# Reordering the first head pair's units, another split of a division, two copies on ScalarE and larger adds on GpSimd in an attention and gate kernel

## Chip, cores and metric

One core of a Trainium2 chip. The metric is device microseconds of one execution, read as the median of several. Profiles give spans from the first to the last recorded instruction, which are about 2 us shorter than the time.

## The reference

```python
xn = layernorm(x)                                # x: 2048 x 640, bf16
q  = (xn @ wq)                                   # 32 heads of 192
s  = softmax(q @ k[-512:].T * 192**-0.5) @ v[-512:]   # per head, the last 512 cached positions
s  = s.reshape(2048, 32*192) @ wo
g  = silu((silu(xn @ w_gate) * (xn @ w_up)) @ w_down)
return x + s * g
```

## The kernel before

The gate `g` is computed first. Then the 32 heads go in 16 pairs. For each pair there is a phase of queries and scores, and after it a "stretch" of context and output units. The 2,048 rows are four blocks (0 to 3), each with two halves of context, `a` and `b`. The names in the order below are: `2a0` is the first half-unit of block 2's context half `a`; `2w`, `2x` and `2y` are output projections done in block 2's place, of the block two places earlier: first two row tiles, last two row tiles, and the rest columns of all four. `0e` is one query unit. Below, `w` and `x` units are called row units and `y` units rest units. Accumulators (`mm` and `sc` in the timelines) are the PSUM buffers that a unit's matmuls write and VectorE or ScalarE empties.

```python
def pv(i, q2):                     # context of block i, half q2
    ...
            st["acc"] = sc_tile() if i < 2 and q2 else mm_tile()   # two buffers each
    ...
            if p == 3:
                divide(i, q2, acc, (0, 1) if i < 2 and q2 else ())  # by VectorE, else ScalarE

def divide(i, q2, acc, by_dve):
    nc.vector.reciprocal(r[:], ...)
    ...                             # O_b = acc * r, on VectorE or ScalarE
    nc.sync.dma_start_transpose(out=OT_b[:, 6*q2 : 6*q2+6, :], in_=O_b[:, 2*q2 : 2*q2+2, :, :])

def sum_rows(i, qts, sc):          # end of a row unit
    ...
    add_sum(pr, to, sc)            # first pair: copy out of PSUM on VectorE; later: add

FIRST = """0a0 0b0 0a1 0b1 0e0 1b0 1a0 1b1 2b0 1a1 2b1 2w0 2x0 2w1 2a0 2x1 2a1 2y0 3a0 3y0 3a1 3x0
    3b0 3x1 3w0 3b1 3w1"""
...                                 # before the last pair's end: x onto the sums, on GpSimd
for qt in range(4):
    add_x(n, slice(qt, qt + 1))
add_x(n)
```

A projection needs the transposed context `OT_b` of the block that it projects: `2w` needs what half `a` of block 0 gave, `2x` what half `b` gave, `2y` both.

The softmax here doesn't subtract the row's maximum and nothing guards it: scores larger than these inputs give would overflow.

## Time and profile before

| | before |
|---|---|
| time, first three runs | 922.93 us (922.89 to 923.27) |
| span of the profiled execution | 921.8 us |
| TensorE busy | 914.7 us, 99% |
| VectorE, ScalarE, GpSimd busy | 65%, 51%, 10% |
| first pair's stretch (first context half-unit to the next query unit) | 190.74 to 210.40: 19.66 us |

A timeline row has the start, the length, the engine, the source line, the operation, output and input, how many instructions it merges, and in brackets how long the engine sat idle before it and what ended that. Matmul rows overlap, since their ends are modelled. So work is sized from start to start. Idle time of an engine other than TensorE costs nothing by itself. The rows of before stand in the prediction.

### The profile page before, as it was taken

How to read it: one execution, taken by the hardware profiler on the slowest of the kernel's cores; microseconds unless marked ns; L12 is line 12 of the kernel's file. 1: busy time of each engine (PE TensorE's matmuls, PEld its weight loads, DVE VectorE, ACT ScalarE, POOL GpSimd, SP SyncE). 2: the span in 40 equal slices, each digit the busy share in tenths (PEclk: the TensorE clock that was granted, in tenths of full speed). 3: DMA queues.
4: the chain of work that ended last, by engine and by line, in shares of the span. 5: the costliest groups of instructions: out<-in, count | busy, mean ns of one | idle time of the engine just before them, and what ended most of it. 6: DMA issues, size and time to landing. Idle time of an engine off the chain costs nothing.

```text
span 921.8 us, 23762 instructions
## 1 busy us (share of the span) xinstructions
PE 914.7 (99%) x10193; PEld 527.3 (57%) x10193; DVE 594.6 (65%) x844; ACT 473.7 (51%) x841; POOL 91.0 (10%) x302
## 2 busy tenths in 40 slices
PE   9999999999999999999999999999999999999998
PEld 5444445564747464656565656565656565555664
DVE  6443321467676777777777767676767676767656
ACT  4222222546464656565655565655556565556561
POOL 0000000000000000000000000000000000002977
PEclk9999999999999999999999999999999999999999
DMA  9312430045443425343534453435353434333535
GB/s 310 68 34 65 90 78 1 1 67 121 51 112 47 111 56 104 58 103 58 108 58 108 57 109 57 97 58 97 69 95 65 92 75 76 89 70 108 127 48 163
DMA packets 246969, 77.45 MB, mean 84 GB/s; under 512 B 227792, under 2 KB 246864, under 8 KB 246864
## 3 DMA queue, kind: packets, MB, share of 16 engines
q1 hardware_dynamic: 245376, 74.23, 39.3%
q8 instruction: 80, 1.31, 0.6%
q10 hardware_dynamic: 1488, 1.70, 0.6%
q14 instruction: 25, 0.20, 0.1%
HBM read 39.06 MB, written 2.62 MB: 45 GB/s over the span
## 4 chain that ended last, share of the span: by engine, by line
PE 98%; DMA 1%; DVE 0%; SPq 0%; POOLq 0%; POOL 0%; issue 0%; DVEq 0%
PE mm L460 22%; PE sc L474 18%; PE sc L619 16%; PE mm L499 16%; PE sc L282 11%; PE mm L321 6%; PE sc L587 3%; PE sc L579 2%; PE mm L551 2%; PE mm L579 1%; DMA x_t<-in_A_x_dram 1%; DMA OT_b<-O_b 1%; PE gu L282 0%; PE mm L330 0%; PE sc L551 0%; PE sc L499 0%
## 5 line engine op out<-in xcount | busy, mean ns | idle before, releaser
L478 ACT ACTIVATE p_t<-sc 128x1024 bf16<-128x1024 f32 x254 | 253.3, 1024 | 120.2 <-PE sc L474 120.2
L465 DVE TENSOR_REDUCE qT<-mm 128x512 bf16<-128x1024 f32 x189 | 231.2, 1223 | 98.9 <-PE mm L460 96.4
L529 ACT ACTIVATE O_b<-mm,r 128x192 bf16<-128x192 f32 x490 | 166.5, 423 | 190.4 <-issue 138.9
L460 PE MATMUL mm<-xnT,wq_p 64*128 64x512 bf16 x1890 | 234.9, 376 | 0.0
L474 PE MATMUL sc<-qT,khat 64*128 64x512 bf16 x1524 | 195.4, 376 | 0.0
L619 PE MATMUL sc<-wo_p,OT_b 64*128 64x512 bf16 (+1 forms) x1608 | 179.2, 345 | 1.2 <-DMA OT_b<-O_b 1.2
L499 PE MATMUL mm<-V_p,p_t 64*128 64x193 bf16 x3520 | 178.3, 242 | 0.0
L499 PEld LDWEIGHTS <-p_t 64*128 64x128 bf16 x3584 | 155.0, 93 | 34.6
L460 PEld LDWEIGHTS <-wq_p 64*128 64x128 bf16 x1890 | 91.8, 94 | 112.0 <-issue 0.7
L632 DVE TENSOR_TENSOR s_m<-s_m,sc 128x1024 f32<-128x1024 f32 x82 | 100.2, 1222 | 49.3 <-PE sc L619 43.0
L474 PEld LDWEIGHTS <-khat 64*128 64x128 bf16 x1536 | 74.8, 94 | 91.0
L619 PEld LDWEIGHTS <-OT_b 64*128 64x128 bf16 x1608 | 75.6, 94 | 46.2 <-DMA OT_b<-O_b 1.7
L605 POOL MEMSET turn_t<- 128x1 f32 x246 | 24.4, 99 | 699.1 <-PE mm L499 494.2
L290 DVE TENSOR_TENSOR hT<-sc,sg 128x512 bf16<-128x512 f32 x46 | 31.7, 692 | 81.6 <-ACT sg L289 81.6
L632 DVE TENSOR_TENSOR s_t<-s_t,sc 128x512 f32<-128x512 f32 x82 | 56.2, 686 | 18.3 <-PE sc L587 16.8
L289 ACT ACTIVATE sg<-sc 128x512 bf16<-128x512 f32 x46 | 27.4, 597 | 69.7 <-PE sc L282 68.2
L282 PE MATMUL sc<-xnT,wg_sb 128*128 128x512 bf16 (+1 forms) x260 | 60.2, 354 | 0.1
L282 PE MATMUL sc<-xnT,wu_sb 128*128 128x512 bf16 (+1 forms) x260 | 60.2, 354 | 0.0
L632 DVE TENSOR_TENSOR s_o<-s_o,sc 128x640 f32<-128x640 f32 x52 | 42.7, 821 | 15.9 <-PE sc L619 14.8
L321 PE MATMUL mm<-wd_sb,hT 128*128 128x512 bf16 (+1 forms) x240 | 46.7, 347 | 0.0
L518 DVE RECIPROCAL r<-mm 128x4 f32<-128x4 f32 x124 | 22.6, 182 | 33.1 <-PE mm L499 24.7
L282 PEld LDWEIGHTS <-wu_sb 128*128 128x128 bf16 x285 | 27.0, 98 | 27.1 <-issue 0.3
(94 smaller groups left out, 458.9 us busy)
## 6 DMA issues: line engine op xcount, KB each, us to landing
wo_p<-in_A_wo_dram SPq DMA_DIRECT2D x16, 480.0 KB, 4.9
K_p<-in_A_k_cache_dram SPq DMA_DIRECT2D x32, 192.0 KB, 4.6
V_p<-in_A_v_cache_dram SPq DMA_DIRECT2D x32, 192.0 KB, 3.1
wq_p<-in_A_wq_dram SPq DMA_DIRECT2D x64, 80.0 KB, 2.9
wq_p<-in_A_wq_dram SPq DMA_DIRECT2D x16, 160.0 KB, 3.2
x_t<-in_A_x_dram SPq DMA_DIRECT2D x14, 160.0 KB, 3.1
OT_b<-O_b SPq DMA_TRANSPOSE x124, 2.7
wd_sb<-in_B_w_down_dram SPq DMA_DIRECT2D x1, 1920.0 KB, 11.8
```

The lines of the kernel that those rows point to most:

```text
L282: nc.tensor.matmul(out, w_sb[:, c, f * P : (f + 1) * P], xnT[:, c, qc], start=(c == 0), stop=(c == NC - 1),)
L290: nc.vector.tensor_tensor(hTs[b][:, f, :], u, sg[:], ALU.mult)
L321: nc.tensor.matmul(dn, at, by, start=(f == 0), stop=(f == NF - 1))
L460: nc.tensor.matmul(q_ps[:, h, :], pairs[pr]["wq"][r, c, j * P : (j + 1) * P], xnT[r, c, b * 512 : (b + 1) * 512], start=(c == 0), stop=(c ...
L465: nc.vector.reduce_sum(qTs[i][:, j, :], q_ps[:, :, :].rearrange("p h n -> p n h"), axis=AX.X)
L474: nc.tensor.matmul(sc[:, h, :], khat[r, j, ks], qT[r, j, :], start=(j == 0), stop=(j == 2))
L478: nc.scalar.activation(p_t[:, :, :], sc[:, :, :], ACT.Exp, scale=scale)
L499: m = nc.tensor.matmul(acc[:, k, h * 256 : h * 256 + Dh + 1], Ps[i][kc][r, h, qt * P : (qt + 1) * P], V_p[r, kc, h, 0 : Dh + 1], start=(p ...
L529: nc.scalar.activation(O_b[:, qt, h, :], a_k[:, h, 0:Dh], ACT.Copy, scale=r[:, k, h, :])
L579: nc.tensor.matmul(ps, OTs[i][:, 3 * qt + j, :], pairs[i // NB]["wo"][:, j, cols], start=(first and j == 0), stop=(end and j == 2),)
L619: m = nc.tensor.matmul(ps[:, k, 0 : cols.stop - cols.start], OTs[i][r, 3 * qt + j, :], pairs[i // NB]["wo"][r, j, cols], start=(turn == 0 ...
L632: nc.vector.tensor_tensor(to, to, ps, ALU.add)
```

## The change

The intent is to have more work between a context half and the projection that needs its transpose, and to spread what empties the accumulators over VectorE and ScalarE. The matmuls stay the same, 10,193.

```diff
-                divide(i, q2, acc, (0, 1) if i < 2 and q2 else ())
+                divide(i, q2, acc, (0, 1) if q2 == i else ())
...
-        add_sum(pr, to, sc)
+        if i < 2 and qts.start:
+            nc.scalar.copy(to, sc)
+        else:
+            add_sum(pr, to, sc)
...
-    FIRST = """0a0 0b0 0a1 0b1 0e0 1b0 1a0 1b1 2b0 1a1 2b1 2w0 2x0 2w1 2a0 2x1 2a1 2y0 3a0 3y0 3a1 3x0
-        3b0 3x1 3w0 3b1 3w1"""
+    FIRST = """0a0 0b0 0a1 0b1 0e0 1a0 1b0 1a1 2a0 1b1 2a1 2w0 2b0 2w1 2b1 2y0 2x0 3a0 2x1 3w0 3a1 3w1
+        3x0 3b0 3x1 3b1 3y0"""
...
-                            for qt in range(4):
-                                add_x(n, slice(qt, qt + 1))
+                            for qt in (0, 2):
+                                add_x(n, slice(qt, qt + 2))
```

## The prediction

> **What bounds the kernel now.** I read the page's first part, then TensorE's waits, the chain that ended last and the timeline, and only then the other engines around the gap that these showed. The page's busy line, then all of TensorE's matmul waits:
>
> ```profile
> PE 914.7 (99%) x10193; PEld 527.3 (57%) x10193; DVE 594.6 (65%) x844; ACT 473.7 (51%) x841; POOL 91.0 (10%) x302
> ```
>
> ```profile
> PE sc L619 <- DMA OT_b<-O_b: 1.2, 1, 1.2
> PE gu L230 <- DVE zero_t L179: 1.2, 1, 1.2
> PE tp L344 <- DVE xn L267: 0.2, 1, 0.2
> ```
>
> TensorE is busy for 914.7 of 921.8 us, and the mean granted clock is 1.000. Only one wait lies in the middle: an output projection waited for a transposed context tile, once. The other two belong to the start. So this change can win about that wait and no more. The chain there (start, length, what):
>
> ```profile
> 195.32 0.57 PE mm L499 x13
> 195.89 4.62 DMA OT_b<-O_b
> 200.51 0.05 issue
> 200.55 1.47 PE sc L619 x12
> ```
>
> and TensorE's timeline over the same microseconds:
>
> ```profile
> 195.82 0.83 PE L499 MATMUL sc<-V_p,p_t 64*128 64x193 bf16 x16
> 196.49 2.17 PE L499 MATMUL mm<-V_p,p_t 64*128 64x193 bf16 x48
> 198.49 0.81 PE L619 MATMUL sc<-wo_p,OT_b 64*128 64x512 bf16 x6
> 200.55 1.47 PE L619 MATMUL sc<-wo_p,OT_b 64*128 64x512 bf16 x12 [1.25 <-DMA OT_b<-O_b]
> 201.86 0.83 PE L499 MATMUL mm<-V_p,p_t 64*128 64x193 bf16 x16
> ```
>
> Rows overlap by the modelled ends, so I size units by start to start: 16 context matmuls 0.67 us, 6 projection matmuls 0.65 us, and 10 query matmuls 1.08 us (the chain's lengths). The unit that began at 198.49 should have been followed at 199.14; the next began at 200.55. Loss 1.41 us. Check by the whole stretch of the first pair, from 190.74 to 210.40: 19.66 us for 16 context half-units (10.67), 10 projection half-units (6.47) and one query unit (1.08), together 18.22. The difference is 1.44 us, so this is the only gap in the stretch. The later pairs repeat every 46.96 us in the chain (232.79, 279.75, 326.71 ...), with no wait listed.
>
> Why was the transpose late? The transposes took this long to land, and the second, issued at 195.89, is the 4.6:
>
> ```profile
> DMA to landing us min/median/max: 2.7/2.8/4.6
> ```
>
> The transfer rate from 198.5 to 200.0 in 40 slices (busy tenths of the 16 engines, GB/s):
>
> ```profile
> DMA  0000000000000101001010010010049999999999
> GB/s 0 0 0 0 0 0 0 7 7 7 7 7 7 14 7 14 7 7 14 7 14 7 7 14 7 7 14 7 14 102 273 259 287 280 294 214 267 300 287 287
> ```
>
> A trickle of about 7 GB/s until 199.6: nearly all of the tile had moved before 198, and one straggler finished late. The one instruction packet of these microseconds (queue q8, 0.02 MB) moves just before 198.
>
> **What the Trainium skill says.** "Runtime: NRT & Kernel Launch", Instruction fetch mechanics, says that instructions are streamed by DMA in 16 KiB blocks while the engine runs; the page's 80 instruction packets with 1.31 MB agree in size (16 KB each). "DMA: Bandwidth & Descriptors", Queues, rings and completion order, says that each DMA engine alternates between its queues packet by packet: a 16 KB packet ahead of small transpose packets on one engine would make this tail. The trace fits, but does not prove it. "VectorE: DVE Perf Modes", The TRN2 errata, gives ScalarE 172 cycles plus one per element from PSUM at 1.2 GHz; for 1,024 columns that is an estimate of 1.00 us. The exponentials of that shape in this trace take 1.024 us, so I use 1.02 for the moved copies; VectorE's take 1.22. "GPSIMD Engine Reference", section 3.1, charges a GpSimd instruction a dispatch beside its per-element cost, so fewer, larger adds are cheaper. The trace agrees: 1.11 us start to start for 512 columns, 2.1 for 1,024.
>
> **The change, part by part.** No matmul is added or removed (the instruction lists have the same length). Four things move.
>
> (1) Order. Before, the second half of block 0's context was needed at 199.14, two projection half-units of 0.65 us before the next block's. Now the rest unit, which needs it first, stands after two more half-units of context and one more of projection. Laying the new list from 190.74 with the sizes above: 1a at 194.49, 1b 195.16, 2a1 ends 198.49, first projection (needs the first half) 198.49, 2b0 199.14, 2w1 199.81, 2b1 200.46, rest unit 201.12, second row unit 201.77, stretch over at 208.97. The second half is divided by ScalarE: VectorE first does the first half (reciprocal 192.95, two products to 194.18), so the second's reciprocal ends at 194.39, ScalarE needs 1.36, and the transpose is issued at about 195.8, as before. Landed after 2.8 us: 198.6; after 4.6 again: 200.4. Wanted at 201.12. The gap of 1.41 goes even if the straggler stays.
>
> (2) VectorE divides the first half of block 0 instead of the second. The next user of that accumulator starts at 194.49; VectorE is done at 194.18, ScalarE would be at 194.52. Cost 0, margin 0.3.
>
> (3) Two of the four row copies (1.22 us on VectorE) go to ScalarE (1.02 us each). ScalarE is idle there; VectorE loses 2.44 us of work. Nothing on the path, but buffers matter. The second row unit reuses the bank pair of the first; VectorE's copy of the first starts 0.20 us after its slot ends (before: slot end 201.86, copy 202.06), so 200.66 to 201.88, plus 0.05 to release TensorE. Wanted at 201.77. New wait: 0.16 us. After that shift the next reuse (rest unit's copy and add on VectorE, to about 203.5) is wanted at 203.89, fine. The last one (second rest unit: copy and add 209.33 to 210.75) is wanted by the second scores of the next pair at 210.86: margin 0.06 us after the release, so 0 to 0.1 us.
>
> (4) GpSimd adds x in four instructions of 1,024 columns instead of eight of 512:
>
> ```profile
> 880.30 4.50 POOL L657 TENSOR_TENSOR s_m<-s_m,x_b 128x512 f32<-128x512 f32 x4
> 885.86 4.50 POOL L657 TENSOR_TENSOR s_m<-s_m,x_b 128x512 f32<-128x512 f32 x4
> 890.31 1.16 POOL L657 TENSOR_TENSOR s_t<-s_t,xT 128x512 f32<-128x512 f32 x1
> 896.74 2.35 POOL L719 TENSOR_TENSOR x_b<-s_f,s_m 128x1024 bf16<-128x1024 f32 x1 [5.26 <-DVE s_f L718]
> ```
>
> Two large ones took 4.21 us for the same shape of multiply, so 0.29 is saved twice, 0.6 us. But GpSimd then idles 5.26 us for VectorE: worth 0.
>
> Sum: 1.41 - 0.16 - 0.05 = 1.2 us saved; 922.93 - 1.2 = 921.7.
>
> **Rivals.** *The gap belongs to the profiled run only.* The profiled execution took 923.57, the timed ones 922.93. With the usual 2.8 us the old transpose would land at 198.7, before 199.14, and there would be nothing to win: the change would leave 923.0 or 923.1. For it: a straggler is chance. Against: instruction packets come at fixed places of the program. I give it one in five. *A new wait takes the old one's place.* The bank reuse at 201.77 or the accumulator at 194.49 could cost more than I reckon, if VectorE runs late: each slip of VectorE's queue by 0.3 us costs at most that. It would make 922.0 to 922.5. The straggler could also hit another transpose, but every other one has over 0.6 us of slack. *The GpSimd adds were in the end's chain.* Its last step is a GpSimd add, but the 5.26 us of idle time before say no. If the idle reading were wrong, 0.6 us more would go: 921.1. *A bound of another kind* (a 2% change is 18 us) would need a stage that today has no wait at all to stall repeatedly; the later pairs are untouched.
>
> **Range and chances.** Weighing 921.7 against the one in five for 923.0, I predict 921.8. The range 921.0 to 922.9 holds no change at its top and the gap plus half the GpSimd time at its bottom. All of it is within 2%: chances 0.005 faster, 0.99 same, 0.005 slower.
>
> **What would show it.** Right: TensorE's waits lose the wait on the context transpose; the first pair's stretch is 18.3 to 18.5 us instead of 19.66; a short wait of 0.1 to 0.2 us on VectorE's copy stands before the second row unit; ScalarE's two copies show about 1.02 us; GpSimd's adds are done earlier and its idle time before the final adds grows by that. Wrong: the transpose wait stays or another of its size appears there; the stretch is short but the time isn't (then the gap never was in the timed runs); or the last chain after TensorE's end changes length.

## The result, and the profile after

The changed kernel took 921.67 us (median of six runs, 921.56 to 922.19), the kernel before 922.98 us in the same rounds (922.75 to 923.27). The ratio is 0.9986, with a 95% interval of 0.9973 to 0.9999: "same" at the threshold of 2%. A ratio here is the mean time of one kernel's fast runs over that of the other's of the same rounds, so it is not quite the ratio of the medians.

TensorE's waits in the changed kernel, all of them (waiting, releaser, total us, times, longest):

```profile
PE gu L230 <- DVE zero_t L179: 1.2, 1, 1.2
PE sc L282 <- ACT xnT L350: 0.3, 1, 0.3
```

The wait on the transpose is gone. Both lines that are left lie in the first microseconds. TensorE's timeline of the changed kernel from the first projection on, whose counterpart are the rows from 198.49 in the prediction:

```profile
197.88 0.81 PE L619 MATMUL sc<-wo_p,OT_b 64*128 64x512 bf16 x6
198.53 0.83 PE L499 MATMUL mm<-V_p,p_t 64*128 64x193 bf16 x16
199.20 0.81 PE L619 MATMUL sc<-wo_p,OT_b 64*128 64x512 bf16 x6
199.84 0.83 PE L499 MATMUL mm<-V_p,p_t 64*128 64x193 bf16 x16
200.51 0.81 PE L587 MATMUL sc<-OT_b,wo_p 64*128 64x512 bf16 x6
201.33 0.82 PE L619 MATMUL sc<-wo_p,OT_b 64*128 64x512 bf16 x6
201.97 0.85 PE L499 MATMUL mm<-V_p,p_t 64*128 64x193 bf16 x16
```

The starts follow each other at 0.65 and 0.67 us, except for one: the rest unit at 200.51 should have been followed at 201.16, and the second row unit began at 201.33. That is a wait of 0.17 us which the table of waits does not list; only the starts show it. What it waited for is VectorE's copy of the first row unit, which ends at 200.05 + 1.22 = 201.27:

```profile
200.05 1.22 DVE L630 COPY s_m<-sc 128x1024 f32<-128x1024 f32 x1 [1.30 <-PE sc L619]
```

The stretch runs from 190.13 to 208.53: 18.40 us. Before it was 19.66, so 1.26 us went there. The transpose itself is as late as ever. This is the second one, issued at 195.1, in the changed kernel:

```profile
L532 SPq DMA_TRANSPOSE OT_b<-O_b x1: 1217/1217/1217, 195.1 to 195.1; - x1
...
DMA to landing us min/median/max: 4.6/4.6/4.6
```

It lands at about 199.7, 0.8 us before the rest unit wants it. ScalarE's moved copies and GpSimd's adds in the changed kernel:

```profile
203.50 1.01 ACT L641 COPY s_m<-sc 128x1024 f32<-128x1024 f32 x1 [0.75 <-PE sc L619]
207.43 1.01 ACT L641 COPY s_m<-sc 128x1024 f32<-128x1024 f32 x1 [0.99 <-PE sc L619]
```

```profile
878.43 4.21 POOL L660 TENSOR_TENSOR s_m<-s_m,x_b 128x1024 f32<-128x1024 f32 x2
883.71 4.21 POOL L660 TENSOR_TENSOR s_m<-s_m,x_b 128x1024 f32<-128x1024 f32 x2
...
894.87 2.35 POOL L722 TENSOR_TENSOR x_b<-s_f,s_m 128x1024 bf16<-128x1024 f32 x1 [5.83 <-DVE s_f L721]
```

The two groups of adds take 4.21 us instead of 4.50, and GpSimd's idle time before the final adds grew from 5.26 to 5.83, as the prediction asked for.

**The spans differ by more than the times.** 921.8 - 919.5 is 2.3 us, the times differ by 1.3. The traces divide the 2.3 us into three. The first context half-unit started at 190.13 instead of 190.74: 0.61 us, because in the profile of before a tile of x landed at 8.32 us instead of 7.23, and TensorE's work on it began at 10.54 instead of 9.94. This start varies from run to run; in the thirteen other profiles of any kernel it lay between 190.1 and 191.4. The stretch gave 1.26. From its end to the last TensorE piece of the chain, nothing changed (703.84 and 703.85 us from the query unit to the start of that piece). The rest, 0.43 us, lies after TensorE's end, where the prediction saw nothing. There the clear of GpSimd's closing starts 5.88 us after the chain's last TensorE piece in both kernels; what differs comes after it. First before, then after (count, durations in ns, first and last start):

```profile
L875 POOLq DRAIN  x3: 78/182/1101, 917.5 to 921.4; - x3
...
L875 POOLq EVENT_SEMAPHORE_RANGE_CLEAR  x1: 96/96/96, 920.9 to 920.9; - x1
```

```profile
L878 POOLq DRAIN  x3: 39/78/1094, 915.7 to 919.2; - x3
...
L878 POOLq EVENT_SEMAPHORE_RANGE_CLEAR  x1: 96/96/96, 919.1 to 919.1; - x1
```

Before, the last drain comes 0.3 us after the clear has ended and takes 182 ns. After, it follows within 0.1 us and takes 39 ns. The experiments below ask why.

### The profile page after: what moved, and what is told of

Read it like the earlier page. It is cut to its first block, busy times and chain, and to the rows that moved or that the text cites. A ratio compares the mean times of both kernels' runs of the same rounds, so it can differ in the third digit from the quotient of the medians.

```text
span 919.5 us, 23759 instructions
## 1 busy us (share of the span) xinstructions
PE 914.1 (99%) x10193; PEld 565.6 (62%) x10193; DVE 592.2 (64%) x842; ACT 474.3 (52%) x843; POOL 90.2 (10%) x298
## 3 DMA queue, kind: packets, MB, share of 16 engines
q8 instruction: 80, 1.31, 0.6%
## 4 chain that ended last, share of the span: by engine, by line
PE 99%; DVE 0%; POOLq 0%; POOL 0%; issue 0%; ACT 0%; DVEq 0%
PE mm L460 22%; PE sc L474 18%; PE sc L619 16%; PE mm L499 16%; PE sc L282 11%; PE mm L321 6%; PE sc L587 3%; PE sc L579 2%; PE mm L551 2%; PE mm L579 1%; PE gu L230 1%; PE gu L282 0%; PE mm L330 0%; PE sc L551 0%; PE sc L499 0%; PE mm L474 0%
## 5 line engine op out<-in xcount | busy, mean ns | idle before, releaser
L529 ACT ACTIVATE O_b<-mm,r 128x192 bf16<-128x192 f32 x486 | 164.6, 421 | 184.0 <-issue 138.4
L460 PE MATMUL mm<-xnT,wq_p 64*128 64x512 bf16 x1890 | 237.5, 376 | 0.0
L474 PE MATMUL sc<-qT,khat 64*128 64x512 bf16 x1524 | 198.0, 376 | 0.0
L619 PE MATMUL sc<-wo_p,OT_b 64*128 64x512 bf16 (+1 forms) x1608 | 182.1, 345 | 0.0
L499 PE MATMUL mm<-V_p,p_t 64*128 64x193 bf16 x3520 | 181.4, 242 | 0.0
L499 PEld LDWEIGHTS <-p_t 64*128 64x128 bf16 x3584 | 160.9, 93 | 28.8
L460 PEld LDWEIGHTS <-wq_p 64*128 64x128 bf16 x1890 | 105.0, 94 | 98.7 <-issue 0.7
L474 PEld LDWEIGHTS <-khat 64*128 64x128 bf16 x1536 | 85.3, 94 | 80.4 <-DVE s_t L632 0.3
L619 PEld LDWEIGHTS <-OT_b 64*128 64x128 bf16 x1608 | 85.8, 94 | 37.3 <-issue 0.3
```

The source lines that it names most:

```text
L460: nc.tensor.matmul(q_ps[:, h, :], pairs[pr]["wq"][r, c, j * P : (j + 1) * P], xnT[r, c, b * 512 : (b + 1) * 512], start=(c == 0), stop=(c ...
L474: nc.tensor.matmul(sc[:, h, :], khat[r, j, ks], qT[r, j, :], start=(j == 0), stop=(j == 2))
L499: m = nc.tensor.matmul(acc[:, k, h * 256 : h * 256 + Dh + 1], Ps[i][kc][r, h, qt * P : (qt + 1) * P], V_p[r, kc, h, 0 : Dh + 1], start=(p ...
L529: nc.scalar.activation(O_b[:, qt, h, :], a_k[:, h, 0:Dh], ACT.Copy, scale=r[:, k, h, :])
L619: m = nc.tensor.matmul(ps[:, k, 0 : cols.stop - cols.start], OTs[i][r, 3 * qt + j, :], pairs[i // NB]["wo"][r, j, cols], start=(turn == 0 ...
```

## The experiments

The theory: the only thing that costs time in the kernel before is that the second transpose lands late behind an instruction packet, and the order takes this off the path. Rivals: the copies, the division or the adds bring the gain; or the delay has another cause. In the table, "stretch" is read from each run's timeline, "tail" is from the end of the chain's last TensorE piece to the span's end (the spans taken to 0.01 us from the traces), and times are medians, beside the kernel before in the same rounds. A dash means one execution only.

| run | stretch | tail | time | before |
|---|---|---|---|---|
| before | 19.66 | 6.71 | | 922.98 |
| changed | 18.40 | 6.28 | 921.67 | 922.98 |
| order alone | 18.49 | 6.72 | 922.29 | 923.40 |
| all but the order | 19.07 | 6.28 | 922.74 | 923.40 |
| before, 144 empty instructions | 18.23 | 6.72 | 922.30 | 923.40 |
| before, 36 empty instructions | 18.77 | 6.91 | - | |
| division alone | 19.34 | 6.73 | 922.77 | 923.32 |
| copies and adds alone | 19.72 | 6.28 | - | |
| changed, old division | 18.50 | 6.29 | - | |
| changed, copies on VectorE | 18.40 | 6.28 | - | |
| changed, old adds | 18.39 | 6.71 | 922.38 | 923.40 |
| changed, third context buffer | 18.41 | 6.27 | 922.20 | 923.40 |
| changed, three fixes | 18.24 | 6.29 | 921.56 | 923.40 |
| changed, 4 empty GpSimd instructions | 18.39 | 6.71 | 922.54 | 923.32 |

Stretches agree between runs to 0.01 us where nothing waits on the transposes. The medians scatter by some 0.4 us, mostly from the start. So parts under half a microsecond are judged by the stretch.

### The order alone

```diff
 kernel before
+    FIRST = (the new order)
```

> The kernel before with the new order of units alone (old division, all copies on VectorE, old adds on GpSimd). Theory (the order removes the wait for the late transpose, the rest of the change only trims waits for buffers): the first pair's stretch, from the first context half-unit to the first query unit of the next pair, falls from 19.66 us to about 18.5 (18.22 of work, 0.17 of waiting for VectorE's copy before the second row unit as in the changed kernel, about 0.1 because the first accumulator is now emptied by ScalarE); time about 1.1 us under the kernel before, 921.9. Rival (the ScalarE copies or the GpSimd adds bring the gain): 923.0, stretch 19.6.

Measured: ratio 0.9987 (0.9974 to 0.9999), 1.1 us under the kernel before; stretch 190.14 to 208.63, 18.49 us. It is what the theory said to 0.01 us, and both small waits are there: block 1's first context unit starts 0.08 us late, and the row unit 0.17 us late after the rest unit:

```profile
200.61 0.83 PE L587 MATMUL sc<-OT_b,wo_p 64*128 64x512 bf16 x6
201.43 0.82 PE L619 MATMUL sc<-wo_p,OT_b 64*128 64x512 bf16 x6
```

So the order brings the gain, nearly all of it.

### Everything but the order

```diff
 changed kernel
+    FIRST = (the old order)
```

> The changed kernel with the old order of units (new division, two copies by ScalarE, new adds). Theory: the wait on the transposed context tile comes back, 1.2 us on TensorE, stretch 19.5 to 19.7, time 922.9 to 923.0, no gain. Rival (copies or adds matter): 921.7 to 922.4.

Measured: ratio 0.9993 (0.9980 to 1.0005), 0.66 us under. The wait is back as the theory said, but smaller:

```profile
200.09 1.47 PE L619 MATMUL sc<-wo_p,OT_b 64*128 64x512 bf16 x12 [0.66 <-DMA OT_b<-O_b]
```

By starts it is 0.82 us instead of 1.41, and the transpose landed in 4.2 us. This was a miss, and led to the two runs on its parts below.

### Is it the instruction packet?

In slices of a profile one sees the one packet of the instruction queue. In the kernel before, from 197.8 us in slices of 0.01 us (GB/s), it is the 1664 at 197.88:

```profile
GB/s 102 51 77 51 26 51 51 26 1664 26 0 0 0 0 0 0 0 0 0 0 0 0 0 0 0 0 0 0 0 0 0 0 0 0 0 0 0 0 0 0
```

The trace's record of this packet lasts from 197.88 to 198.80. A transpose is 768 packets of 256 B there. Of the second one's, 502 had moved from 197.08 to 197.9; then nothing moved until 198.79; then 30 came one behind the other, never more than two at a time, until 199.6 (the trickle shown in the prediction); the last 236 moved after that at full rate. So a third of the tile, and not one straggler, was late. Empty instructions in TensorE's stream are meant to shift where its blocks end; the program's own work stays the same.

```diff
 kernel before, in the loop over the gate layer's tiles
                 if b or f >= 4:
                     ffn_hidden(b, f)
+                if b:
+                    for _ in range(4):              # 36 passes: 144 empty instructions
+                        nc.tensor.nop(nofuse=True, hint="pad")
```

> The kernel before, order and all, with 144 empty instructions added to TensorE's stream during the gate layers, where its sequencer has time. This moves the boundaries of the instruction blocks 144 instructions earlier, so the instruction packet that moved at 197.9 us would move about 3 us earlier, before the first two transposes. Theory (the straggler of the second transpose waits behind that packet on one engine): the second transpose lands after 2.8 us instead of 4.6, TensorE's wait on it is gone without any reordering, stretch 18.2 to 18.3, time about 1.4 us under the kernel before, 921.6, unless the empty instructions cost something themselves outside the stretch. Rival (transposes close together delay each other, or the second is slow for its own reasons): landing stays 4.6, wait stays, 923.0.

Measured: ratio 0.9984 (0.9971 to 0.9998), 1.1 us under by the medians, 1.4 by the means. The packet moved to 193.7, 4.3 us earlier against the first context unit, and its record ends at 194.86, before any transpose's data moves. The second transpose landed in 2.8 us, the wait is gone, and the old order runs without a gap: eighteen matmuls in one row, followed 1.94 us later by the next unit.

```profile
198.64 2.10 PE L622 MATMUL sc<-wo_p,OT_b 64*128 64x512 bf16 x18
200.58 0.83 PE L502 MATMUL mm<-V_p,p_t 64*128 64x193 bf16 x16
```

The next packet came at 200.5, on the heels of the third transpose, issued at 198.1, and it was that one which now took 4.4 us:

```profile
L535 SPq DMA_TRANSPOSE OT_b<-O_b x1: 1212/1212/1212, 198.1 to 198.1; - x1 
...
DMA to landing us min/median/max: 4.4/4.4/4.4
```

Nobody needs it soon. The control with a quarter of the empty instructions:

```diff
-                    for _ in range(4):
+                    for _ in range(1):              # 36 empty instructions
```

> Control for the run with 144 empty instructions: the kernel before with 36 of them. The instruction packet should move about 0.75 us earlier, from 197.9 to about 197.1, which is the beginning of the second transpose's data instead of its end. Theory (the packet's place decides): the second transpose still lands late, 4.2 to 4.7 us, and TensorE still waits, 0.8 to 1.5 us; stretch 19.0 to 19.7. Rival (empty instructions by themselves took the wait away): no wait, stretch 18.2.

Measured: the packet moved further than I reckoned, to 195.4 us, which is 2.0 us earlier against the first context unit instead of 0.75. (I counted 48 instructions per microsecond, which also gave 3 us instead of 4.3 for the run before, and cannot say what the rest is; in the kernels without empty TensorE instructions too the packet lay between 6.2 and 7.1 us after the first context unit.) There it met the first two transposes: they landed in 4.2 and 3.7 us instead of 2.8 and 4.6. The first projection started 0.32 us late and the next unit 0.22, together the 0.54 us by which the stretch exceeds 18.23:

```profile
198.40 2.32 PE L622 MATMUL sc<-wo_p,OT_b 64*128 64x512 bf16 x18 [0.16 <-DMA OT_b<-O_b]
```

The stretch missed its range on the low side, so this control is only half of one: the empty instructions did change the wait, but through the packet's place. The DMA records of all fourteen traces settle more. They hold 1,736 context transposes, 124 in each; most take about 2.75 us, and 348 took 3.65 us or more. During 334 of those 348 a packet of queue q8 was under way. The other 14 are one in each trace, issued near 905 us, when output is being written. The packet's place decides: where one began 1.0 to 2.2 us after the issue, 204 of 213 transposes were that late; with none under way, 14 of 962. So the packet is the cause. The delay is not rare either: in the kernel before, 22 of the 124 were that late, but only this one shows a wait of TensorE. That the trickle is the queue of one DMA engine fits its one-by-one packets, but the records do not name the engine.

### Which part shortened the wait in the old order?

```diff
 kernel before
+        the two copies on ScalarE and the four large adds, old order, old division
```

> The kernel before with only the two copies on ScalarE and the large GpSimd adds; old order, old division. The run with everything but the order waited 0.82 us instead of 1.41, which I had not expected. Theory: that part came with the division (its second half then is issued 0.2 us earlier against TensorE and lands sooner behind the packet), so here the wait is again 1.3 to 1.5 us and the stretch 19.6 to 19.7. Rival (the copies shortened it): wait 0.8, stretch 19.1.

Measured, in one profile: the unit that should have followed at 198.59 started at 200.06, a wait of 1.47 us, stretch 19.72. So the copies and adds do nothing here.

```profile
200.06 1.47 PE L619 MATMUL sc<-wo_p,OT_b 64*128 64x512 bf16 x12 [1.31 <-DMA OT_b<-O_b]
```

```diff
 kernel before
-                divide(i, q2, acc, (0, 1) if i < 2 and q2 else ())
+                divide(i, q2, acc, (0, 1) if q2 == i else ())
```

> The kernel before with only the new division (VectorE divides the first half of block 0, ScalarE the second), old order, copies and adds. Theory from the last runs: the run with everything but the order waited 0.82 us and the one with copies and adds alone 1.47, so the division is worth about 0.6: wait 0.7 to 1.0 us, stretch 18.9 to 19.2, time 0.5 to 0.7 us under the kernel before. Rival (the packet's place varied between those two single profiles): wait 1.3 to 1.5, stretch 19.5 to 19.7, time within 0.2 us of the kernel before.

Measured: ratio 0.9992 (0.9979 to 1.0006), 0.55 us under by the medians; wait by starts 1.10 us, stretch 19.34.

```profile
199.71 1.47 PE L619 MATMUL sc<-wo_p,OT_b 64*128 64x512 bf16 x12 [0.94 <-DMA OT_b<-O_b]
```

This lies between the two forecasts. The time speaks for the division, the trace for a smaller effect; the interval includes no effect. With the packet moving by some tenths of a microsecond from run to run, what the division is worth in the old order stays open, between 0.3 and 0.6 us. One part of it is steady: all eight profiles with the new division issue the second transpose 4.95 or 4.96 us after the first context unit, the six with the old one 5.14 or 5.15. So 0.2 us comes from the earlier issue. In the new order it is a matter of one buffer only, as the next run shows.

### The changed kernel with one part undone

```diff
 changed kernel
-                divide(i, q2, acc, (0, 1) if q2 == i else ())
+                divide(i, q2, acc, (0, 1) if i < 2 and q2 else ())
```

> The changed kernel with the old division (ScalarE divides the first half, VectorE the second). Theory: the first context unit of block 1 waits about 0.08 us for ScalarE to empty the accumulator, as in the run with the order alone; stretch 18.48 instead of 18.40. Rival (the division matters more, through the transposes): stretch over 18.6.

Measured: stretch 18.50; block 1's first unit starts at 194.09 instead of 192.93 + 1.08 = 194.01. As expected, 0.08 us.

```diff
 changed kernel
-        if i < 2 and qts.start:
-            nc.scalar.copy(to, sc)
-        else:
-            add_sum(pr, to, sc)
+        add_sum(pr, to, sc)
```

> The changed kernel with all four row copies on VectorE. By my sum the stretch stays 18.40 and the second scores of the next pair wait 0.07 us at most for VectorE; the run with the order alone showed none. So the copies' move is worth 0.0 to 0.1 us. Rival (the moved copies matter): stretch 18.6 or more.

Measured: stretch 18.40, and the second query unit 2.38 us after the first, against 2.37 with the copies on ScalarE. The copies' move is worth nothing.

```diff
 changed kernel
-                            for qt in (0, 2):
-                                add_x(n, slice(qt, qt + 2))
+                            for qt in range(4):
+                                add_x(n, slice(qt, qt + 1))
```

> The changed kernel with the old adds of x, eight of 512 columns instead of four of 1,024. Theory: GpSimd's two groups take 4.50 us instead of 4.21 each, its idle time before the final adds shrinks from 5.83 to about 5.3 us, and nothing else moves: same time as the changed kernel (stretch 18.40, end after TensorE's last matmul unchanged). Rival (the adds are on the path to the end): 0.6 us longer.

Measured: ratio 0.9988 (0.9975 to 1.0000), 1.0 us under the kernel before; stretch 18.39; groups of 4.50 us and 5.29 us of idle time. The adds are off the path as expected. But the tail is 6.71 us again. By now all traces fell in two classes: the old adds with tails of 6.7 to 6.9 us, the new adds with 6.27 to 6.29, whatever else was changed. The last issue of an output transfer came 3.54 us after the chain's last TensorE piece both before and after, so it is not the adds' own time. GpSimd's stream is four instructions shorter with the new adds: the traces hold 579 instead of 583 (the next expectation counts one more in each, and by TensorE's last matmul it means the chain's last TensorE piece).

```diff
 changed kernel, near the start
+    for _ in range(4):
+        nc.gpsimd.nop(nofuse=True, hint="pad")
```

> The changed kernel with four empty instructions on GpSimd near the start, so that its stream is as long as before the change (584 instructions instead of 580), with the new large adds kept. Found in all traces so far: with the old adds the span ends 6.7 to 6.9 us after TensorE's last matmul, and GpSimd's closing drain takes 182 ns and comes some 0.4 us after the step before it; with the new adds 6.2 to 6.3 us, 39 ns and under 0.1. Theory A (the number of GpSimd instructions, that is where its last ones stand in its instruction blocks): here the long closing drain and the 6.7 us are back. Theory B (the form or size of the adds): 6.3 us and a short drain, as in the changed kernel. Either way the stretch is 18.40, and the difference between time and span, 2.1 to 2.2 us with the new adds and 1.8 to 1.9 with the old, goes with it, so the time moves by 0.2 us at most.

Measured: ratio 0.9989 (0.9977 to 1.0002); stretch 18.39; tail 6.71 us, and the long closing drain is back:

```profile
L880 POOLq DRAIN  x3: 78/183/1097, 916.8 to 920.6; - x3
```

So theory A holds: the tail goes with the number of GpSimd's instructions, not with the adds. Whether the last ones then stand past the end of an instruction block stays open: no instruction packet moves between the clear and the last drain in any trace. Little of the 0.43 us reaches the time: time less span is 1.84 us (median) in this run and 1.83 with the old adds, but 2.08 to 2.16 in the timed runs with the short tail. About 0.3 us of the shorter span is given back outside of it; 0.15 us may remain.

### Can the last wait go too?

```diff
 changed kernel
+    order after 2y0:  3a0 2x0 3a1 2x1 3w0 3b0 3w1 3x0 3b1 3x1 3y0
+    if i == 2: the context output O_b gets a buffer of its own (so ScalarE need not wait for the late transpose)
```

> The changed kernel with its last wait taken away: a third buffer for the context output of block 2 (so ScalarE divides it without waiting for the late transpose) and the order after the rest unit changed so that a context half-unit stands before the second row unit, which gives VectorE's copy 0.67 us more. Theory: the 0.17 us before the second row unit goes, stretch 18.22 to 18.3 instead of 18.40, time about 0.15 us under the changed kernel, 921.5, within the scatter of runs. Rival (another buffer binds at once): stretch 18.4 or more.

Measured: ratio 0.9987 (0.9974 to 1.0000); stretch 18.41. The wait before the second row unit is gone, but the rival won: ScalarE's copies now stood behind its divisions, block 1's second row unit started 0.17 us late, and the next pair's first scores 0.36 us late:

```profile
210.16 1.47 PE L474 MATMUL sc<-qT,khat 64*128 64x512 bf16 x12 [0.19 <-ACT s_m L644]
```

```diff
 the kernel of that run
-                divide(i, q2, acc, (0, 1) if q2 == i else ())
+                divide(i, q2, acc, (0, 1) if q2 == i or (i == 3 and q2) else ())
-        if i < 2 and qts.start:
+        if i == 1 and qts.start:
             nc.scalar.copy(to, sc)
```

> The run with the third context buffer, mended: there ScalarE's copies stood behind its divisions and made two new waits of 0.17 and 0.36 us. Now VectorE copies block 0's second rows, and divides the last half of block 3, so ScalarE is free for the one copy left. Theory: no wait in the stretch nor in the next scores: stretch 18.22 to 18.25, the second query unit of the next pair 2.37 us after the first; time about 0.15 to 0.2 us under the changed kernel, hard to see in timed runs. Rival (yet another buffer binds): stretch 18.35 or more.

Measured: ratio 0.9979 (0.9965 to 0.9992); stretch 191.19 to 209.43, 18.24 us, the second query unit 2.37 us after the first. No wait is left in it. The median, 921.56, is 0.8 us under the run with the old adds of the same rounds. The stretch explains 0.15 of that and the tail at most 0.43; the rest is within the scatter of the start. It is the best version here on every measure that the traces give, by 0.16 us over the changed kernel; the two were not timed side by side.

## Why the prediction was right

- **The gap of 1.41 us is the prize, and the order takes it.** Right. Order alone gave 1.17 us of stretch, the whole change 1.26.
- **It goes even if the straggler stays.** Right. The second transpose still took 4.6 us in the changed kernel, and landed 0.8 us ahead of need.
- **A new wait of 0.16 us for the accumulator bank.** Right: 0.17. Its size came from the copy's length and the 0.20 us between a unit's end and its copy, both read before the change.
- **The first accumulator, margin 0.3 us.** Right: VectorE's products ended at 193.57 and TensorE took the buffer at 193.88. With ScalarE, the miss is 0.08 us.
- **The second scores, 0 to 0.1 us.** It was 0.01 at most.
- **ScalarE's copies 1.02 us.** 1.01; the estimate from "VectorE: DVE Perf Modes", The TRN2 errata, was 1.00. They are worth nothing; VectorE had the time.
- **GpSimd's adds worth 0.** Right for the adds. The step overlooked that four instructions fewer shorten the closing of GpSimd's stream, 0.43 us of the span and perhaps 0.15 of the time. The prediction had named a changed length after TensorE's end as a sign of being wrong, and this sign came.
- **One straggler, with nearly all of the tile moved before 198.** Misread: a third of the tile moved after 199.6, and 22 transposes of that kernel are late. The sum did not rest on it, only on the landing time; and no other late transpose shows a wait, as the prediction said.
- **The rival that the gap belongs to the profiled run only.** Refuted: order alone won 1.1 us in five runs.
- **The division, with the second transpose issued "as before".** Too simple: it is issued 0.2 us earlier, and in the old order the new division shortened the wait in both profiles that had it, to 0.82 and 1.10 us. By how much for good is open.

The sum was 1.2 us, with 921.7 as the outcome if the gap was real, and 921.8 after weighing. Measured: 1.31 us and 921.67. That these agree so closely is partly luck: the sum left out the shorter closing, the medians scatter by some 0.4 us, and the same kernel with the old adds won 1.0 us. The stretch, 18.40 us against a forecast of 18.3 to 18.5, is the firmer agreement.

## What to carry to other kernels

When one engine is busy for 99% of the span, size the change by the gaps between its starts, unit by unit; the table of waits showed each about 0.16 us shorter than the starts did (1.25 against 1.41), so one of 0.17 was missing from it. A transfer whose median looks short can still be late now and then, beside an instruction packet: give the consumer some 2 us of slack, or see whether a few empty instructions move the packet off it. When a part is said to be off the path, look at what it does to instruction counts too, and compare times and not spans.

## What the Trainium skill lacked or had wrong

- "Runtime: NRT & Kernel Launch", Instruction fetch mechanics, calls the cost of crossing a block boundary "mostly hidden". It was hidden for TensorE's own stream, but the packet delayed a transpose of this kernel from 2.8 us to 4.2 to 4.7 us, and TensorE by up to 1.47 us through it.
- "DMA: Bandwidth & Descriptors", Queues, rings and completion order, has the alternation between queues by packets, but no figure for what an instruction packet does to a small transfer: here 204 of 213 transposes with such a packet beginning 1.0 to 2.2 us after their issue took 3.65 us or more, instead of about 2.75.
- "GPSIMD Engine Reference" says nothing on the closing of its stream: in the seven traces with 583 instructions the last drain took 173 to 183 ns, in the seven with 579 it took 34 to 39 ns, and the span was 0.43 us shorter after TensorE's end.
